# Loading r, k and v of the first four blocks as pairs of tokens in a fused time-mixing and feed-forward kernel

## The chip, the cores and the metric

The kernel runs on one core of a Trainium2 chip, in one launch. The metric is device time in microseconds (us): the median of several executions, lower is better. A profile is one further execution, recorded by the hardware profiler. Its span runs from the first to the last recorded instruction, and its own device time is a little longer than the span.

The engines are named as in the profile: PE does matrix multiplies (PEld loads their stationary operand), DVE is the vector engine, ACT the scalar engine, POOL the general-purpose one. SP computes nothing here; it issues most of the transfers (DMA) in the order of its own queue.

## The reference, cut to what matters

For each of 4 batches (index `j` in the kernel) and 8 heads there are 768 tokens with 48 channels a head. A recurrence over the tokens gives y, its rows are laid side by side over the heads to x (3072 rows of 384), and a gated feed-forward with 1536 hidden units follows.

```python
for t in range(S):                        # r, k, v, w: (4, 8, 768, 48); u: (8, 48)
    cur = einsum('bhd,bhe->bhde', u[None] * k[:, :, t], v[:, :, t])
    y[:, :, t] = einsum('bhd,bhde->bhe', r[:, :, t], state + cur)
    state = w[:, :, t][..., None] * state + einsum('bhd,bhe->bhde', k[:, :, t], v[:, :, t])
x = y.transpose(0, 2, 1, 3).reshape(B * S, H * D)
xn = x / sqrt(mean(x * x) + 1e-6) * rms_g
out = (silu(xn @ w_gate) * (xn @ w_val)) @ w_out
```

All inputs are float32 in HBM; the matrix multiplies of before take bfloat16 operands, but for two small ones (`u_mm`, `g_mm`), and add in float32.

## The kernel before, in words

**Blocks.** The work is cut into 24 blocks `(n, j)`: block `n` (0 to 5) of 128 tokens of batch `j` (0 to 3). Each block goes through the recurrence in chunked form. With the logarithms of w summed over the tokens of the block (`ln`, `cs_mm`), r is scaled by the exponential of the sum (`exp_r`, `r_mul`) and k by that of its negative (`exp_k`, `k_mul`). Both are transposed (`rk_pe` on PE and `rk_tr`, or, for n of 2 and more, `rk_tr` alone as a transposing DMA), scores of all token pairs are formed (`q_mm`, even heads in one PSUM bank and odd heads in another), masked to earlier tokens (`q_mask_e`, `q_copy_o`, `q_mask_o`), and y is scores times v plus r times the state from before the block (`y_mm`). `st_mm` and `st_new` make the new state. The term with u, which concerns a token itself, is made on the side: `bonus_mul` (two POOL multiplies), `bonus_sum` (DVE), `bonus_v` (POOL), which leaves the tile `ydiag`; `x_add` (DVE, L553) adds it to y out of PSUM into the tile `xb`. Then x is normed (`x_sq`, `x_rstd`, `xn_mul`), transposed (`xn_pe` and `xn_out`, or `xn_tr` and `xn_gain`) and waits in a tile `xnt`.

**Feed-forward groups.** Four blocks make a group of 512 rows: `gate_mm`, `silu`, `val_mm`, `h_mul` for each of 12 slices of the hidden units, then `o_mm`, `o_out`, `out_dma` for each of the four blocks. The first group consists of the blocks (0,0), (0,1), (1,0) and (1,1), so its first matrix multiply (L617) has to wait for these four blocks to be through. The later groups overlap with the recurrence of later blocks.

**Loads.** `load` (L259) brings r, k or v of one block into a tile of 128 partitions (tokens) by 8 heads by 48 channels: 192 KB, in 1024 runs of 192 bytes, since tokens lie 192 bytes apart within one head. Eight such tiles a tensor (`NIN`) rotate. `load_w` (L271) does the same, but for the blocks in the set `WIN` (n of 0 and 1, all four batches) it loads the 256 tokens of two blocks at once: partition p holds tokens 2p and 2p+1, in 1024 runs of 384 bytes. Sums over tokens then take two matrix multiplies, with two masks cut from `mw` (L404, L408, L411). r, k and v of those blocks are still laid out one token a partition. All loads, the transposing DMAs and the stores of the result go through SP's queue; the weights of the feed-forward (`load_gv`, `load_wo`) through POOL's.

**Order.** Nothing is reordered at build time. A text, `ORDER`, lists every step as `step.n.j`, and each engine runs its instructions in that order, waiting where an operand or a buffer is not there. A number behind a colon puts that many multiplies by a tile of zeros ahead of the step (L238 on three 128-column transposes each, L240 on 384 columns); their results are overwritten, and they fill time on PE. PSUM is split into two banks `a`, two banks `b` and four banks `q`; the function `psum` gives a step the bank whose last use lies furthest back. Sets such as `CAST_ACT`, `K_POOL`, `RK_DVE`, `ODD_DVE` and `OUT_DVE` say for each block which engine does a step.

Of the kernel before, what the change touches and what calls it, by code (L numbers as in the profile page):

```python
# [30 lines left out]
bonus_mul.1.0 q_mask_e.0.0 load_k.1.3 load_r.1.2 load_k.1.2 load_r.1.3 load_v.1.2 bonus_mul.0.1 load_w.2.1 load_w.2.0
load_v.1.3 load_w.2.3 q_mm.1.0:2 cs_mm.1.1 exp_r.1.1 exp_k.1.1 r_mul.0.1 k_mul.0.1 w_tot.0.1 q_mask_o.1.0
bonus_sum.1.0 load_gv.0.1 cast_v.0.1 load_r.2.0 bonus_sum.0.1 r_mul.1.1 load_w.2.2 rk_pe.0.1:2 ln.0.3 y_mm.0.0
rk_tr.0.1 st_mm.0.1:4 x_add.0.0 q_mask_e.1.0 st_new.0.1 cs_mm.0.3:3 bonus_v.0.1 cast_v.1.0 q_mm.0.1:1 y_mm.1.0
k_mul.1.1 bonus_v.1.0 cast_v.1.1 q_copy_o.0.1 x_sq.0.0 bonus_mul.1.1 load_r.2.1 x_add.1.0 exp_r.0.3 load_r.2.2
x_sq.1.0 load_r.2.3 load_k.2.0 q_mask_e.0.1 w_tot.1.1 rk_pe.1.1:1 rk_tr.1.1 q_mm.1.1:7 q_mask_o.1.1 load_gv.0.0
q_mask_o.0.1 y_mm.0.1:8 g_mm.0.0 bonus_sum.1.1 ln.0.2 x_rstd.1.0 xn_mul.1.0 x_rstd.0.0 xn_mul.0.0 exp_k.0.3
bonus_v.1.1 load_gv.1.0 q_mask_e.1.1 x_add.0.1 x_sq.0.1 x_rstd.0.1 y_mm.1.1 x_add.1.1 k_mul.0.3 xn_pe.1.0:2 xn_pe.0.0
cs_mm.0.2 g_out.0.0 xn_out.1.0 x_sq.1.1 xn_mul.0.1 xn_out.0.0 r_mul.0.3 st_mm.1.1:3 x_rstd.1.1 st_mm.1.0 xn_mul.1.1
xn_pe.0.1 xn_out.0.1 w_tot.0.3 rk_pe.0.3:3 xn_pe.1.1 xn_out.1.1 exp_r.0.2 exp_k.0.2 r_mul.0.2 val_mm.0.0:4 gate_mm.0.3  # L40
silu.0.3 val_mm.0.3 rk_tr.0.3 w_tot.0.2 st_new.1.1 load_gv.1.1 k_mul.0.2 bonus_mul.0.2 q_mm.0.3 h_mul.0.3 st_new.1.0
gate_mm.0.2 gate_mm.0.0 rk_pe.0.2 silu.0.0 silu.0.2 val_mm.0.2 q_mask_e.0.3 h_mul.0.0 gate_mm.0.5 gate_mm.0.1 silu.0.5
silu.0.1 val_mm.0.1 rk_tr.0.2 q_copy_o.0.3 h_mul.0.1 bonus_mul.0.3 bonus_sum.0.3 h_mul.0.2 gate_mm.0.6:1
gate_mm.0.11:1 q_mm.0.2 cast_v.0.2 silu.0.6 silu.0.11 q_mask_o.0.2 gate_mm.0.8 val_mm.0.6 q_mask_e.0.2 cast_v.0.3
st_mm.0.2 val_mm.0.11 q_mask_o.0.3 h_mul.0.6 val_mm.0.5 y_mm.0.3 y_mm.0.2 bonus_sum.0.2 bonus_v.0.2 load_wo.0.0
# [668 lines left out]
```

## Time and profile before

| | us |
|---|---|
| median of 3 runs (203.16 to 204.44) | 204.01 |
| the profiled execution, device time | 203.96 |
| its span | 202.2 |
| PE busy in it | 191.3 (95%) |
| DVE busy | 157.5 (78%) |
| ACT busy | 135.0 (67%) |
| POOL busy | 124.4 (62%) |

A line of the timeline gives start and duration in us, the engine, the source line, the operation, `out<-in` and how many instructions were merged into it; brackets at its end say how long the engine sat idle before it and for whom. Matrix multiplies are pipelined, so the time that one takes is read from the start of one line to the start of the next. In the table by stages each engine's entry is its busy time, with the number of instructions in brackets. SPq is SP's queue of transfers; its line starts when SP begins to issue.

### The profile page before, as it was taken

To read this page: it belongs to the slowest core of one execution; us is meant where nothing else is said; L and a number is where in the kernel's file an instruction comes from. 1 tells how busy PE (TensorE), PEld (TensorE's weight loads), DVE (VectorE), ACT (ScalarE), POOL (GpSimd) and SP (SyncE) were. 2 spreads that over 40 slices of the span, in tenths; PEclk is the share of its full clock that TensorE was granted. 3 is DMA by queue.
4 is the path that set the end of the run, shared out by engine and by line. 5 is a ranking of instruction groups with operands and counts; after the bars stand their busy time and mean duration, and the time that the engine had idled before them with its cause. 6 is when DMAs were issued, how large, how long until landed. Compare 5 with 4: busy or idle time off the path is not lost.

```text
span 202.2 us, 4604 instructions
## 1 busy us (share of the span) xinstructions
PE 191.3 (95%) x1677; PEld 121.9 (60%) x1694; DVE 157.5 (78%) x307; ACT 135.0 (67%) x278; POOL 124.4 (62%) x178
## 2 busy tenths in 40 slices
...
GB/s 144 231 234 207 212 208 202 195 179 208 206 184 225 160 212 191 210 185 188 199 176 215 237 188 203 183 190 108 134 179 104 0 23 99 0 117 0 63 115 99
DMA packets 121567, 32.42 MB, mean 160 GB/s; under 512 B 116420, under 2 KB 120392, under 8 KB 121544
## 3 DMA queue, kind: packets, MB, share of 16 engines
...
q10 hardware_dynamic: 8, 0.00, 0.0%
...
## 4 chain that ended last, share of the span: by engine, by line
PE 65%; ACT 3%; DMA 2%; DVE 2%; issue 1%; SPq 0%; DVEq 0%; ACTq 0%
PE ps_av L617 7%; PE ps_bu L617 7%; PE ps_au L617 7%; PE ps_bv L617 6%; PE ps_qx L660 6%; PE ps_qv L660 6%; PE ps_qu L660 5%; PE ps_qz L660 4%; PE ps_au L622 2%; PE ps_bu L622 2%; DMA rkT<-rk 2%; PE ps_av L622 2%; PE ps_bv L622 2%; ACT L249 1%; PE ps_au L419 1%; PE ps_qv L500 1%
## 5 line engine op out<-in xcount | busy, mean ns | idle before, releaser
L660 PEld LDWEIGHTS <-ht 128*128 128x128 bf16 x300 | 28.1, 98 | 17.5 <-DVE ht L646 1.0
L251 ACT ACTIVATE sg<-ps_av 128x512 bf16<-128x512 f32 x36 | 21.5, 597 | 22.8 <-PE ps_av L617 18.0
L646 DVE TENSOR_TENSOR ht<-ps_bv,sg 128x512 bf16<-128x512 f32 x29 | 19.9, 687 | 13.9 <-PE ps_bv L617 12.9
L251 ACT ACTIVATE sg<-ps_au 128x512 bf16<-128x512 f32 x36 | 21.5, 596 | 11.5 <-PE ps_au L617 7.7
L617 PEld LDWEIGHTS <-wg_sb 128*128 128x128 bf16 x180 | 19.2, 114 | 15.9 <-issue 0.6
L617 PEld LDWEIGHTS <-wv_sb 128*128 128x128 bf16 x180 | 19.2, 114 | 15.7 <-issue 0.5
L465 POOL TENSOR_TENSOR ruk<-rt,kt 128x384 f32<-128x384 f32 x24 | 24.0, 1001 | 3.7 <-DMA kt<-in_k_dram 2.8
L475 POOL TENSOR_TENSOR ydiag<-vt,diag 128x384 f32<-128x384 f32 x24 | 20.4, 859 | 9.4 <-DVE diag L470 9.1
L617 PE MATMUL ps_av<-xnt,wg_sb 128*128 128x512 bf16 x88 | 25.0, 381 | 0.3
L466 POOL TENSOR_TENSOR ruk<-ruk,u_bc 128x384 f32<-128x384 f32 x24 | 24.0, 1001 | 1.9
L617 PE MATMUL ps_bu<-xnt,wv_sb 128*128 128x512 bf16 x86 | 24.8, 380 | 0.4
L646 DVE TENSOR_TENSOR ht<-ps_bu,sg 128x512 bf16<-128x512 f32 x31 | 21.3, 686 | 4.8 <-PE ps_bu L617 3.1
L617 PE MATMUL ps_au<-xnt,wg_sb 128*128 128x512 bf16 x87 | 23.6, 380 | 0.1
L617 PE MATMUL ps_bv<-xnt,wv_sb 128*128 128x512 bf16 x82 | 23.2, 380 | 0.2
L459 POOL TENSOR_TENSOR rk<-kt,ek 128x384 bf16<-128x384 f32 x16 | 15.9, 1001 | 9.7 <-ACT ek L251 5.9
L249 ACT ACT_TABLE_LOAD x14 | 18.0, 1283 | 1.9 <-PEq L698 1.6
L660 PE MATMUL ps_qx<-wo_sb,ht 128*128 128x384 bf16 x96 | 17.1, 326 | 0.2 <-DVE ht L646 0.2
L558 ACT ACTIVATE junk<-xb 128x384 bf16<-128x384 f32 x24 | 12.5, 522 | 6.3 <-DVE xb L553 6.2
L571 ACT ACTIVATE xn<-xb,rstd 128x384 bf16<-128x384 f32 x24 | 14.2, 609 | 0.6 <-POOL rstd L567 0.5
L470 DVE TENSOR_REDUCE diag<-ruk 128x8 f32<-128x384 f32 x24 | 13.1, 544 | 1.9 <-POOL ruk L466 1.9
L660 PE MATMUL ps_qv<-wo_sb,ht 128*128 128x384 bf16 (+1 forms) x84 | 13.8, 314 | 0.0
L251 ACT ACTIVATE lw<-wt 128x384 bf16<-128x384 f32 (+1 forms) x20 | 11.6, 583 | 2.8 <-DMA wt<-in_w_dram 2.7
...
## 6 DMA issues: line engine op xcount, KB each, us to landing
rt<-in_r_dram SPq DMA_DIRECT2D x24, 192.0 KB, 4.0
vt<-in_v_dram SPq DMA_DIRECT2D x24, 192.0 KB, 3.9
kt<-in_k_dram SPq DMA_DIRECT2D x24, 192.0 KB, 3.9
out_dram<-ob SPq DMA_DIRECT2D x23, 192.0 KB, 2.2
wt<-in_w_dram SPq DMA_DIRECT2D x16, 192.0 KB, 3.7
...
```

Of the source, the lines that this page charges most:

```text
L249: nc.scalar.preload_act_table_set(table_name)
L251: return nc.scalar.activation(**kw).ins
L459: eng.tensor_tensor(out=rk[:, n % 2, j, 1, :, 0:D], in0=inp["k", n, j], in1=bank["cs_k", n, j][:, 0:DM].rearrange("p (h d) -> p h d", h=H) ...
L465: nc.gpsimd.tensor_tensor(out=ruk[n, j], in0=inp["r", n, j], in1=inp["k", n, j], op=ALU.mult)
L466: nc.gpsimd.tensor_tensor(out=ruk[n, j], in0=ruk[n, j], in1=u_bc, op=ALU.mult)
L470: nc.vector.tensor_reduce(out=diag[n, j].rearrange("p h o -> p (h o)"), in_=ruk[n, j], axis=mybir.AxisListType.X, op=ALU.add)
L475: nc.gpsimd.tensor_tensor(out=ydiag[n, j], in0=inp["v", n, j], in1=diag[n, j].to_broadcast([128, H, D]), op=ALU.mult)
L571: nc.scalar.activation(out=xn, in_=xb[n, j], func=AF.Copy, scale=rstd[n, j][:, 1:2])
L617: nc.tensor.matmul(ps, lhsT=units(ws, c, f), rhs=x[:, c, :], start=(c == 0), stop=(c == KC - 1))
L622: nc.tensor.matmul(ps[:, i * TS // 2:(i + 1) * TS // 2], lhsT=units(ws, c, f + i), rhs=x[:, c, cols], start=(i == 0 and c == 0), stop=(i = ...
L646: nc.vector.tensor_tensor(out=ht[n][:, f, :], in0=v, in1=sg, op=ALU.mult)
L660: nc.tensor.matmul(ps[:, cols], lhsT=ht[n][:, f, b * L:(b + 1) * L], rhs=wo_sb[:, f, cols], start=(f == 0), stop=(f == FC - 1))
```

## The change

Four blocks, (0,0), (0,1), (1,0) and (1,1), form a set `PAIR`. For them r, k and v are loaded as w was: one transfer of 384 KB for both blocks of a batch, 1024 runs of 384 bytes, partition p holding tokens 2p and 2p+1. Block 0 of such a pair then holds the even tokens and block 1 the odd tokens of all 256. What follows in consequence:

- `cs_mm` uses masks of whole token pairs (`mp`) and, for the sum over a chunk, a column that is one on the chunk's half of the partitions (`chunk_of`).
- `rk_tr` writes both blocks of a batch into one tile `rkTp`, sorted by chunk of 128 tokens. `q_mm` makes scores of one chunk at a time: 16 multiplies with 64 output rows in place of 8 with 128.
- `st_mm` and `y_mm` of chunk n take half of the rows (64 partitions) of both blocks, so 8 multiplies in place of 4 and 16 in place of 8.
- `yd_mm` is new: for these four blocks `ydiag` is added in PSUM by PE, through two float32 multiplies by a 64x64 part of an identity. `x_add` goes away for them; `x_sq` and `xn_mul` read the PSUM bank.
- `out_dma` of these blocks stores 64 even and 64 odd rows: the destination is 2 x 64 rows of 384 in place of 128 rows.

Beside this, r, k and v of all other blocks lie two batches to a tile (four tiles of 384 KB a tensor in place of eight of 192 KB; still one 192 KB transfer a block). Some buffer counts change (`ydiag` 6 to 5, `rkT` 6 to 5 beside two `rkTp`, `xb` 4 to 3, `qts` 3 to 4), `ORDER` is written anew throughout, and so are the sets that place steps on engines. Counted over the whole kernel, PE loses 24 zero multiplies of 384 columns and gains 3 of 128; DVE loses 4 `x_add`, 5 output copies, 2 transposed copies and 3 masks and gains 2 `k_mul`; ACT gains 5 output copies, 3 score copies and 2 transposed copies. The number of activation table loads, of feed-forward multiplies and of SP's steps for other blocks is the same. All transfers of the four blocks are issued by SP in the order `w.0 k.0 r.0 w.0.1 r.1 k.1 w.0.3 v.0 r.0.2 v.1`, where a single number is the batch of a pair.

```diff
-load_r.0.0 load_w.0.0 u_mm.0.0 ln.0.0 load_v.0.0 load_k.0.0 cs_mm.0.0:2 load_r.1.0 load_w.0.1 u_out.0.0 load_k.1.0
-load_k.0.1 load_w.0.3 load_v.0.1 exp_r.0.0 exp_k.0.0 r_mul.0.0 cast_v.0.0 load_r.0.1 bonus_mul.0.0 load_k.1.1
-bonus_sum.0.0 bonus_v.0.0 k_mul.0.0 cs_mm.1.0 load_r.1.1 load_v.1.1 load_v.1.0 load_w.0.2 rk_pe.0.0:2 rk_tr.0.0
-exp_r.1.0 w_tot.1.0 w_tot.0.0 st_mm.0.0 r_mul.1.0 st_new.0.0 q_mm.0.0:4 load_k.0.3 load_r.0.3 load_r.0.2 load_k.0.2
...
+load_w.0.0 ln.0.0 u_mm.0.0:12 u_out.0.0 load_k.0.0 load_r.0.0 bonus_mul.0.0 bonus_mul.1.0 load_w.0.1 load_r.0.1
+load_k.0.1 load_w.0.3 load_v.0.0 load_r.0.2 load_v.0.1 load_v.0.3 cs_mm.1.0 g_mm.0.0 cs_mm.0.0 exp_k.1.0 exp_r.1.0
+load_w.0.2 load_k.0.3 load_k.0.2 load_r.0.3 load_v.0.2 load_k.1.2 k_mul.1.0 r_mul.1.0 rk_pe.1.0:5 load_r.1.2 exp_k.0.0
+exp_r.0.0 k_mul.0.0 r_mul.0.0 w_tot.0.0 ln.0.1 rk_pe.0.0:2 w_tot.1.0 rk_tr.0.0 rk_tr.1.0 bonus_sum.0.0 cs_mm.0.1
+exp_r.0.1 g_out.0.0 r_mul.0.1 w_tot.0.1 exp_k.0.1 k_mul.0.1 cs_mm.1.1 q_mm.0.0 q_mm.1.0 load_v.1.2 load_r.1.3
+load_w.2.1 q_mask_e.0.0 load_k.1.3 bonus_sum.1.0 q_mask_o.0.0 bonus_mul.1.1 exp_k.1.1 k_mul.1.1 ln.0.3 rk_pe.0.1:1
+bonus_v.1.0 bonus_v.0.0 exp_r.1.1 load_w.2.0 q_mask_e.1.0 q_mask_o.1.0 cs_mm.0.3 cast_v.0.0 cast_v.1.0 load_v.1.3
+r_mul.1.1 load_w.2.2 load_w.2.3 load_r.2.1 load_r.2.0 rk_tr.0.1 w_tot.1.1 st_mm.0.0:3 bonus_sum.1.1 st_new.0.0
+load_gv.0.0 bonus_mul.0.1 y_mm.0.0 rk_pe.1.1 yd_mm.0.0 rk_tr.1.1 load_k.2.1 load_r.2.3 q_mm.0.1 x_sq.0.0 load_k.2.0
+q_copy_o.0.1 q_mask_e.0.1 bonus_sum.0.1 x_rstd.0.0 xn_mul.0.0 bonus_v.1.1 y_mm.1.0 cast_v.1.1 q_mm.1.1:1 q_mask_e.1.1
+q_mask_o.1.1 q_mask_o.0.1 cast_v.0.1 ln.0.2 yd_mm.1.0 bonus_v.0.1 load_gv.0.1 y_mm.0.1 exp_r.0.3 st_mm.0.1 st_new.0.1
+x_sq.1.0 x_rstd.1.0 yd_mm.0.1 load_gv.1.0 load_gv.1.1 cast_v.0.3 y_mm.1.1 xn_pe.0.0 yd_mm.1.1 cs_mm.0.2 xn_out.0.0
+w_tot.0.3 x_sq.0.1 xn_mul.1.0 exp_k.0.3 k_mul.0.3 x_rstd.0.1 xn_mul.0.1 xn_pe.0.1 x_sq.1.1 x_rstd.1.1 xn_mul.1.1
+xn_pe.1.0 st_mm.1.1 xn_pe.1.1:3 exp_r.0.2 exp_k.0.2 bonus_mul.0.3 bonus_mul.0.2 r_mul.0.3 xn_out.0.1 xn_out.1.0
+xn_out.1.1 rk_pe.0.3 st_mm.1.0 val_mm.0.2 gate_mm.0.0 w_tot.0.2 r_mul.0.2 k_mul.0.2 gate_mm.0.2 rk_pe.0.2 st_new.1.0
+rk_tr.0.3 silu.0.0 gate_mm.0.1 rk_tr.0.2 cast_v.0.2 silu.0.1 q_mm.0.3 val_mm.0.0 st_new.1.1 bonus_sum.0.2 silu.0.2
+q_mask_e.0.3 h_mul.0.0 q_mask_o.0.3 h_mul.0.2 st_mm.0.3 gate_mm.0.6 gate_mm.0.11 val_mm.0.1 st_mm.0.2 q_mm.0.2
+silu.0.6 silu.0.11 q_mask_e.0.2 val_mm.0.3 gate_mm.0.3 gate_mm.0.8 q_copy_o.0.2 q_mask_o.0.2 h_mul.0.1 bonus_sum.0.3
+bonus_v.0.3 bonus_mul.1.2 silu.0.3 h_mul.0.3 val_mm.0.11 h_mul.0.11 gate_mm.0.5 val_mm.0.6 h_mul.0.6 st_new.0.2
...
+bonus_sum.2.0 out_dma.0.3 rk_tr.2.2 gate_mm.1.0 o_out.0.1 silu.1.0 gate_mm.1.5 st_mm.2.1 val_mm.1.5 gate_mm.1.2
...
-    NIN, NRUK, NYD, NRKT, NE, NXB, NSG, NQT, NHT = 8, 3, 6, 6, 4, 4, 3, 3, 2
+    NIN, NRUK, NYD, NRKT, NE, NXB, NSG, NQT, NHT = 8, 3, 5, 5, 4, 3, 3, 4, 2
+    HL = L // 2
...
+    PAIR = sel("00 01 10 11")
...
+    YD_PE = sel("00 01 10 11")
...
-        inp[which, n, j] = pin.tile([128, H, D], FP32, name=which + "t", bufs=NIN)
+        if (n, j) in PAIR:
+            both = pin.tile([128, 2 * DM], FP32, name=which + "t", bufs=NIN // 2).rearrange("p (h x) -> p h x", h=H)
+            inp[which, 0, j], inp[which, 1, j] = both[:, :, 0:D], both[:, :, D:2 * D]
+            nc.sync.dma_start(out=both,
+                              in_=t[j, :, 0:2 * L, :].rearrange("h (p i) d -> p h (i d)", i=2))
+            return
+        if (which, n, j) not in inp:
+            both = pin.tile([128, 2 * DM], FP32, name=which + "t", bufs=NIN // 2).rearrange("p (b h d) -> p b h d", b=2, h=H)
+            a = j - j % 2
+            inp[which, n, a], inp[which, n, a + 1] = both[:, 0], both[:, 1]
...
+            if (n, j) in PAIR:
+                upto, total = (lambda i, own: mp[:, int(2 * i + 1 - own <= 2 * n)]), (lambda i: chunk_of[:, n:n + 1])
+            else:
+                upto, total = (lambda i, own: mw[:, n, i, own:L + own]), (lambda i: mw[:, n, i, L:L + 1])
...
+        if (n, j) in PAIR:
+            if (0, j) not in rkT:
+                rkT[0, j] = rkT[1, j] = pt.tile([128, 2 * NP, 2, 2, HL], BF16, name="rkTp", bufs=2)
+            out = rkT[n, j][:, :, :, n, :].rearrange("p q c x -> p (q c) x")
+            ps = bank.pop(("tr", n, j)).rearrange("p q (c x) -> p (q c) x", c=2)
...
+            if (n, c) in PAIR:
+                for i in range(NP):
+                    for a in range(2):
+                        for ps, d in ((qe, slice(0, D)), (qo, slice(PD, PD + D))):
+                            nc.tensor.matmul(ps[a * HL:(a + 1) * HL, i, :], lhsT=t[d, NP + i, a, n, :],
+                                             rhs=t[d, i, a].rearrange("p b x -> p (b x)"),
+                                             start=(i == 0), stop=(i == NP - 1))
+                continue
...
+            for m in parts:
+                nc.tensor.matmul(ps[:, i, :], lhsT=pair(rk[rows, m % 2, j, 1], i), rhs=pair(vb[m, j][rows], i),
+                                 start=(not old and i == 0 and m == parts[0]), stop=(i == NP - 1 and m == parts[-1]))
...
+    def yd_mm(n, j):
+        xb[n, j] = bank.pop(("y", n, j))
+        if (n, j) in PAIR:
+            rows = slice(n * HL, (n + 1) * HL)
+            for m in range(2):
+                nc.tensor.matmul(xb[n, j][m * HL:(m + 1) * HL], lhsT=ident32[rows, rows],
+                                 rhs=ydiag[m, j][rows].rearrange("p h d -> p (h d)"), start=False, stop=True)
+            return
+        nc.tensor.matmul(xb[n, j], lhsT=ident32, rhs=ydiag[n, j].rearrange("p h d -> p (h d)"), start=False, stop=True)
...
-        nc.sync.dma_start(out=out[row0:row0 + L, cols], in_=bank.pop(ob)[:, cols])
+        dst = out[row0:row0 + L, cols]
+        if (i, j) in PAIR:
+            dst = dst.rearrange("(x a) m -> a x m", a=2)
+        nc.sync.dma_start(out=dst, in_=bank.pop(ob)[:, cols])
```

More of the change, by code (lines that the diff above doesn't have):

```diff
@@ L31 @@
[L31 to L45, printed above, removed]
@@ new lines @@
+h_mul.0.5 h_mul.0.8 k_mul.1.3 gate_mm.0.7 gate_mm.0.9 rk_pe.1.2 bonus_sum.1.2 bonus_v.1.2 x_add.0.3 rk_tr.1.2
+x_add.0.2 cast_v.1.2 ln.2.1 silu.0.9 silu.0.7 val_mm.0.9 gate_mm.0.4 val_mm.0.4 rk_pe.1.3 rk_tr.1.3 x_sq.0.3 x_sq.0.2
+silu.0.4 q_mm.1.2 cs_mm.2.1 gate_mm.0.10 q_mm.1.3 q_copy_o.1.2 h_mul.0.9 x_rstd.0.2 bonus_mul.1.3 val_mm.0.10
+h_mul.0.4 silu.0.10 h_mul.0.10 val_mm.0.7 h_mul.0.7 q_mask_o.1.2 o_mm.0.2 q_mask_e.1.2 ln.2.0 x_rstd.0.3 xn_mul.0.2
+y_mm.1.2 cs_mm.2.0 cast_v.1.3 q_mask_o.1.3 cs_add.2.1 q_mask_e.1.3 exp_r.2.1 x_add.1.2 o_mm.0.3 y_mm.1.3 xn_pe.0.2
```

253 lines of the change are left out of this document (134 added, 119 removed).

## The prediction

> **What bounds the kernel now.** I read the busy time by stages first, then PE's timeline for what starts the dense stage, then the queue of transfers.
>
> ```profile
> core 0: us, PE busy (x) PEld busy (x) DVE busy (x) ACT busy (x) POOL busy (x), PEclk, DMA share, GB/s
> 0.00:11.00 11.00, 6.84 (x48) 3.93 (x49) 5.46 (x15) 5.13 (x8) 6.22 (x19) 1.00 0.86 187
> 11.00:30.20 19.20, 17.41 (x238) 12.23 (x236) 16.68 (x37) 12.92 (x32) 15.54 (x20) 1.00 1.13 216
> 30.20:199.10 168.90, 167.03 (x1394) 105.72 (x1409) 135.11 (x257) 116.92 (x239) 102.64 (x141) 1.00 0.73 153
> 199.10:202.20 3.10, 0.00 (x0) 0.00 (x0) 0.29 (x1) 0.00 (x0) 0.00 (x0) 0.86 0.28 98
> ```
>
> The stages are mine: 30.2 us is where the first feed-forward multiply starts. From there to 199.1 PE is busy 167.03 of 168.90 us: PE's own work bounds it, and neither a faster load nor a faster DVE shortens it. What can move the time is when that stage starts, whether PE stays fed in it, and the 3.1 us tail. The start, on PE:
>
> ```profile
> 4.16 1.64 PE L372 MATMUL ps_qu<-u_bc,ones_row 1*128 1x384 f32 x2 [4.16 <-POOL ones_row L338]
> 5.74 0.82 PE L240 MATMUL ps_au<-zero 128*128 128x384 bf16 x2
> 6.35 0.85 PE L404 MATMUL ps_au<-lw,mw 128*128 128x384 bf16 x2
> ...
> 7.84 0.84 PE L404 MATMUL ps_av<-lw,mw 128*128 128x384 bf16 x2
> ...
> 14.38 0.50 PE L404 MATMUL ps_av<-lw,mw 128*128 128x384 bf16 x2
> ...
> 15.25 0.50 PE L238 MATMUL ps_qv<-ident,zero 128*128 128x128 bf16 x6
> 15.58 0.61 PE L482 MATMUL ps_qv<-ident,rk 128*128 128x128 bf16 x8
> 16.03 0.36 PE L548 MATMUL ps_qz<-vb,qts 128*128 128x48 bf16 x8
> ...
> 16.96 0.33 PE L528 MATMUL ps_qu<-vb,rk 128*128 128x96 bf16 x4
> 17.13 0.65 PE L240 MATMUL ps_au<-zero 128*128 128x384 bf16 x3
> 17.62 0.49 PE L404 MATMUL ps_au<-lw,mw 128*128 128x384 bf16 x2
> ...
> 18.73 0.23 PE L500 MATMUL ps_qv<-rkT 48*128 48x128 bf16 x1
> ...
> 19.06 0.34 PE L545 MATMUL ps_qx<-st,rkT 128*128 128x96 bf16 x4
> ...
> 20.48 1.30 PE L240 MATMUL ps_qz<-zero 128*128 128x384 bf16 x7
> 22.64 0.23 PE L500 MATMUL ps_qz<-rkT 48*128 48x128 bf16 x1 [0.85 <-DVE rkT L489]
> ...
> 22.97 1.47 PE L240 MATMUL ps_qv<-zero 128*128 128x384 bf16 x8
> ...
> 29.23 0.33 PE L586 MATMUL ps_qz<-ident,xn 128*128 128x128 bf16 x3
> 29.40 0.81 PE L240 MATMUL ps_bv<-zero 128*128 128x384 bf16 x4
> 30.21 0.81 PE L617 MATMUL ps_bv<-xnt,wv_sb 128*128 128x512 bf16 x2
> ...
> 36.94 0.33 PE L240 MATMUL ps_av<-zero 128*128 128x384 bf16 x1
> ...
> 37.74 0.33 PE L240 MATMUL ps_au<-zero 128*128 128x384 bf16 x1
> ```
>
> From 11 to 30.2 us PE is busy too, but much of it is padding: the zero multiplies shown alone (3, 7, 8 and 4 of L240) come to 22 x 0.163 = 3.6 us (three take 17.62 - 17.13 = 0.49). The start waits for loads and for the chain of DVE, ACT and POOL behind them, while PE has room.
>
> ```profile
> 1.31 0.56 SPq L271 DMA_DIRECT2D wt<-in_w_dram  x1
> ...
> 13.51 1.82 SPq L259 DMA_DIRECT2D vt<-in_v_dram  x2
> 15.37 0.70 SPq L271 DMA_DIRECT2D wt<-in_w_dram  x1
> ```
> ```profile
> 8.47 0.50 ACT L387 CAST vb<-vt 128x384 bf16<-128x384 f32 x1
> ```
> ```profile
> 19.11 0.50 POOL L389 CAST vb<-vt 128x384 bf16<-128x384 f32 x1 [0.62 <-DMA vt<-in_v_dram]
> ```
>
> The last two loads of the four blocks are issued from 13.51 us on, and POOL sits waiting for one of them until 19.11 us.
>
> **Term 1, the loads.** Before needs 12 loads of 192 KB and 3 of w (384 KB) until then, 3.5 MB; at the 216 GB/s of the second stage that is 16 us, and with issue and landing it gives the 19. After needs 6 + 3 loads of 384 KB, and `r.0.2` stands ahead of the last: 3.7 MB. Run for run the traffic halves (6144 in place of 12288 for r, k, v). If bytes set the pace, v of batch 1 lands no earlier (19 us); if runs did, in 10 x 1024 of them in place of 15 x 1024 and so at two thirds of the time, it lands at 13. I take 17. But v of batch 0, whose first part is cast at 8.47 us in before, is now eighth in the queue: about half the list, so 13 to 15 us. Loads come 2 us earlier at the end and 6 us later in the middle.
>
> **Term 2, PE's work ahead of the first feed-forward multiply.** Here the change adds to PE. Up to the second `rk_pe`: ACT has w's logarithm at about 5 us, since w is now first in the queue. PE runs 12 zero multiplies at the slow early pace (two take 6.35 - 5.74 = 0.61, so 3.7 us from about 1.1) and `u_mm` (1.6 us): 6.4. The first `cs_mm` takes 7.84 - 6.35 = 1.5 at the slow pace: 8.0; `g_mm` 0.2, the second `cs_mm` 15.25 - 14.38 = 0.87 at full pace, two `rk_pe` of 0.45, and 21 zero transposes of 0.055 (six take 0.33): 1.2. That ends at 11.1 us. Then, until the first feed-forward multiply:
>
> - four `cs_mm` of 0.87: 3.5; three `rk_pe` of 0.45: 1.35; four transposes of xn of 0.17: 0.7; eight zero multiplies: 1.3.
> - four `st_mm`, twice the 17.13 - 16.96 = 0.17: 1.4. Four `y_mm` with 16 multiplies for 8, of 0.025 each: 0.4 each, and 0.17 for the state's part in two: 1.95.
> - four `q_mm`. The 8 of before take 19.06 - 18.73 = 0.33, as two run side by side in two halves of the array's rows. The 16 of after lie in four quarters. If four run side by side they cost 0.33, if only two do 0.66, if none does 1.3. I take 0.6, the case nearest to the row: 2.4.
> - four `yd_mm`, of two float32 multiplies with 384 columns each. The one row of this kind is `u_mm`: 5.74 - 4.16 = 1.58 us at the slow pace, at which bfloat16 took 0.305; halved for the full pace (0.163 for 0.305) it is 0.8. So 1.6 a block and 6.3 for four. The lower end is the bfloat16 multiply's 0.163 (1.3 for all eight). The upper would be 1.58 each, but that needs the slow pace, which the rows from 14 us on exclude, so 0.8 is the upper end too.
>
> The Trainium skill ("FP8 and Floating Point Precision", section TensorE Precision Notes) says that true float32 takes four passes through the array. That would make 4 x 0.163 = 0.65 a multiply and 5.2 us in all, 1.1 less than by the row; the row, 1.58 for 0.305, is 5.2 passes, and has its own start in it.
>
> Sum: 3.5 + 1.35 + 0.7 + 1.3 + 1.4 + 1.95 + 2.4 + 6.3 = 18.9 us, from 11.1 to 30.0; two short waits like those in the rows (0.85 at the longest) I count as 0.6. It starts at 30.6 us, against 30.21: **+0.4 us**. Bounds: with quarter overlap and the lower float32 price PE's list ends 6 us earlier, but then the chain behind the loads holds the start. Its end in before, from that last landing (19.11) to the multiply (30.21), is 11.1 us. After saves four `x_add` from it, of which the chain of one block passes one:
>
> ```profile
> 25.92 0.56 DVE L553 TENSOR_TENSOR xb<-ps_qx,ydiag 128x384 f32<-128x384 f32 x1 [0.30 <-PE ps_qx L548]
> ```
>
> So 17 + 11.1 - 0.56 = 27.5 at the earliest: -2.7. With `q_mm` at 1.3 the list is 2.8 longer: +3.2.
>
> **Term 3, the dense stage.**
>
> ```profile
> rt<-in_r_dram SPq DMA_DIRECT2D x24, 192.0 KB, 4.0
> ```
>
> The program order of both versions, counted by kind, shows the same multiplies left behind the first feed-forward multiply: all of the feed-forward and the recurrence of 20 blocks, with `cs_mm` of (0,3) and (0,2) and `rk_pe` of (0,3) done ahead of it in both. Only the two zero multiplies at 36.94 and 37.74 are gone: **-0.3 us**. DVE loses about 12 instructions and ACT gains 10; at 135 and 117 busy of 169 us neither becomes the bound, and PE's own work covers both. If that cover fails in places, the cost is unknown, since the order is new: from -1.9 (all of PE's idle time gone) to one load waited for in full (4.0 us from issue to landing, the row above). I take 0. The shared tiles for two batches come free later than single ones; the loads they hold back are those of blocks two rounds ahead, so 0 as well, within the same bound. The tail has the same half store at its end: 0, at most 0.4 either way.
>
> **Sum:** 203.96 (the profiled execution; 202.2 of span and 1.8 around it, 0.05 under the median) + 0.4 - 0.3 = 204.1; I forecast **204.2**.
>
> **Rivals.**
>
> *The stores of the four blocks crawl (slower).* The new destination is 2 x 64 rows in place of 128. If the transfer is shared out over engines by its outermost dimension, two engines carry it, not 16.
>
> ```profile
> out_dram<-ob SPq DMA_DIRECT2D x23, 192.0 KB, 2.2
> ...
> u_bc<-in_u_dram ACTq DMA_DIRECT2D x1, 1.5 KB
> g_row<-in_moe_rms_g_dram ACTq DMA_DIRECT2D x1, 1.5 KB
> ```
> ```profile
> GB/s 143 165 259 243 154 187 252 286 298 289 277 265 253 238 226 214 162 123 200 204 164 183 174 263 324 325 310 280 266 253 236 223 230 188 159 199 304 321 326 298
> ```
> ```profile
> q10 hardware_dynamic: 8, 0.00, 0.0%
> ```
> ```profile
> PE ps_qu L500 <- DMA rkT<-rk: 0.6, 1, 0.6
> ```
>
> ACT's queue, q10, carried u (one run) and g (three runs) alone: 8 packets, 4 of data and 4 more. One closing packet for each engine used makes exactly 4 if u used one engine and g three; 16 engines each would have made 32. The best 250 ns anywhere in 2 to 12 us moved 326 GB/s, 20.4 for each of 16 engines. Two engines need 98304 B / 20.4 = 4.8 us for a store that 16 do in 0.6 at that rate: 4.2 us more, in which every later load and transposing DMA, spread over all 16, waits on those two. SP's order puts `rk_tr.2.2`, needed by `q_mm`, right behind the store of (0,3). One such delay fully exposed gives 204.2 + 4.2 = **208.4**; all four 221; none 204.2. It decides once more than 2 us of one store outlast the lead that loads have. For it speaks q10, against it that in before PE waits once, 0.6 us, for a transfer, the last row, so transfers have some lead.
>
> The Trainium skill ("DMA: Bandwidth & Descriptors", section Why a DMA increments its semaphore by 16 and not by 1) states this rule: the engine count is the largest k up to 16 that divides the slowest dimension of both sides. With 2 and 128 that is 2, and with one and three runs it agrees with the 8 packets.
>
> *The start moves with the loads (faster).* If the float32 multiplies and quarters overlap, the start is at 27.5: 203.96 - 2.7 - 0.3 = **201.0**. For it: the last landing is earlier and 24 zero multiplies go. Against: the later v, and PE's list.
>
> *PE's new forms cost more.* `q_mm` without overlap: 204.2 + 2.8 = **207.0**. Against: the rows show two at a time.
>
> *The halved runs do nothing for the landing* (19 us in place of 17): PE's list still covers it, so 204.2 holds.
>
> **How the numbers follow.** Forecast (within 1%, which is about what a measurement here can tell from no change): 0.43, its own range 202.5 to 206. Slow stores 0.37, though part of it is hidden: some of these stay under 207. Dearer forms 0.05. Faster start 0.15. So faster by over 1% 0.15, within 0.43, slower 0.42. The range takes in most of the slow stores and half of the faster case: 201.5 to 209.5.
>
> **What would show it.** Term 1: POOL's or ACT's wait for vt of batch 1 ends near 17 us. Term 2: PE without long idle from 11 us on, `yd_mm` at 1.6 a block, first feed-forward multiply at 30 to 31. Term 3: about 169 us from there to the last output multiply. The slow stores would show as landings near 6 us in place of 2.2 on four stores, and PE waiting for transposed tiles or loads between 55 and 110 us. I am wrong if the first feed-forward multiply comes before 29, or if PE idles over 2 us in the dense stage.

## The result, and the profile after

The changed kernel takes **215.6 us** (median of 4, 213.8 to 216.7) against 204.2 for the kernel before beside it (203.2 to 204.4): 1.056 times as long, 95% interval 1.048 to 1.065. Ratios, here and below, leave out executions more than 1.5% above a kernel's fastest; where several were left out, the spread of all is given. The profiled execution took 216.74 us, its span 214.8, which is 12.6 us more than the span before. The same table by stages as in the prediction, now of the profile after; the second stage ends where the first feed-forward multiply starts:

```profile
core 0: us, PE busy (x) PEld busy (x) DVE busy (x) ACT busy (x) POOL busy (x), PEclk, DMA share, GB/s
0.00:11.00 11.00, 9.71 (x45) 4.59 (x46) 5.38 (x14) 3.28 (x5) 8.41 (x22) 1.00 0.93 254
11.00:34.46 23.46, 22.00 (x320) 15.41 (x317) 14.77 (x34) 17.27 (x39) 18.45 (x23) 0.85 1.09 211
34.46:211.70 177.24, 168.98 (x1395) 106.42 (x1408) 130.59 (x249) 120.61 (x247) 98.42 (x136) 0.99 0.70 138
211.70:214.80 3.10, 0.00 (x0) 0.00 (x0) 0.00 (x0) 0.12 (x1) 0.00 (x0) 0.96 0.19 63
```

Two stages lost time. The feed-forward starts at 34.46 in place of 30.21 (+4.25), and the dense stage takes 177.24 in place of 168.90 (+8.3). PE's idle time in the dense stage rose from 1.9 (168.90 - 167.03) to 8.3 us (177.24 - 168.98); the other 1.9 us are busy time, at a mean clock of 0.99 where before had 1.00. In the second stage the mean clock is 0.85. The waits of PE in the dense stage after (engine and line, what it waited for, us in total, times, longest):

```profile
PE ps_qx L535 <- DMA rkT<-rk: 2.1, 1, 2.1
PE ps_av L441 <- DVE wcol L468: 2.0, 1, 2.0
PE ps_qx L724 <- ACT ob L733: 0.7, 1, 0.7
```

The first, from 79.7 us on, is for a transposed tile. The second, from 125.7 on, is a cumulative sum held up by DVE, which stood waiting for a late load of r. The page of the profile after gives the packets of SP's queue, and the clock in 40 slices:

```profile
PEclk9999958999999999999999996999999999999999
q1 hardware_dynamic: 113208, 28.58, 64.9%
```

The packets count the engines. Before had 119504. The change removes 6144 runs and six transfers on 16 engines (96 closing packets), which leaves 113264; 56 are missing, and 56 = 4 stores x 14. So each of the four new stores used 2 engines, not 16. The records of single packets say the same: the 128 rows of the first of these stores, that of block (1,0), moved from 60.97 to 66.41 us, those of the next two took 4.9 and 4.7 us, while the late stores, with 16 engines, take 0.6. So do the trace's semaphore records: each of the four stores has 3 of them, where a store on 16 engines has 16, and the last of the 3 comes 6.7 to 7.2 us after the issue began.

PEclk's 5 in the sixth slice is new, and so is the 6 at 129 us. The same table of the profile after, now cut at the clock's own steps. PEclk is the third column from the end: 1.00 is full speed and 0.50 half. It also says 1.00 where the trace has no record of the clock; the first record here, at full speed, is at 13.15 us, and what PE did before is read from its rows further down.

```profile
23.39:26.81 3.42, 2.90 (x47) 1.57 (x43) 1.82 (x3) 3.36 (x10) 3.42 (x5) 1.00 1.23 225
26.81:30.22 3.41, 3.41 (x32) 1.46 (x28) 1.56 (x4) 2.60 (x9) 3.15 (x6) 0.50 1.08 162
30.22:33.63 3.41, 3.41 (x31) 2.90 (x30) 1.09 (x3) 2.84 (x5) 2.89 (x4) 0.50 1.12 204
```

For 6.83 us PE ran at half speed, just ahead of the dense stage: 3.4 us of full-speed work. The timeline of PE in the profile after shows it, and what the new forms cost:

```profile
6.89 0.82 PE L428 MATMUL ps_au<-lw,mp 128*128 128x384 bf16 x2
...
13.38 0.61 PE L501 MATMUL ps_qz<-ident,rk 128*128 128x128 bf16 x8
13.82 0.49 PE L428 MATMUL ps_av<-lw,mp 128*128 128x384 bf16 x2
...
15.62 0.24 PE L530 MATMUL ps_qu<-rkTp 48*64 48x128 bf16 x1
...
16.89 0.33 PE L242 MATMUL ps_qu<-ident,zero 128*128 128x128 bf16 x3 [0.63 <-DVE qts L547]
...
20.33 0.86 PE L610 MATMUL ps_qx<-ydiag,ident 64*64 64x384 f32 x4
21.50 0.21 PE L530 MATMUL ps_qu<-rkTp 48*64 48x128 bf16 x1 [0.31 <-ACT rkTp L517]
...
24.48 0.72 PE L601 MATMUL ps_qx<-vb,qts 64*128 64x48 bf16 x16 [0.52 <-ACT vb L407]
...
27.59 1.55 PE L610 MATMUL ps_qu<-ydiag,ident 64*64 64x384 f32 x4
...
34.46 0.84 PE L681 MATMUL ps_bu<-xnt,wv_sb 128*128 128x512 bf16 x2
```

The two multiplies of `cs_mm` take 0.82 us at 6.89 and 0.49 at 13.82, so PE ran slowly until about 13.15. `yd_mm` takes 0.86 us for both of its multiplies at full speed, 1.55 in the slow stretch.

The loads did get faster. The same 3 us, first before, then after:

```profile
5.00:8.00 3.00, 3.00 (x17) 1.24 (x16) 0.62 (x2) 1.32 (x2) 0.92 (x1) 1.00 0.99 200
```
```profile
5.00:8.00 3.00, 2.75 (x14) 1.14 (x14) 0.56 (x1) 0.00 (x0) 1.59 (x5) 1.00 1.17 324
```

200 GB/s became 324. By the packets' records the pair load of v of batch 1 is through at 14.4 us (its landing is recorded at 14.9), where in before POOL waited for a v until 19.11. Nothing in the start waited for it:

```profile
17.26 0.91 ACT L407 CAST vb<-vt 128x384 bf16<-128x384 f32 x2
```

### The profile page after: what moved, and what is told of

Read it like the earlier page. It is cut to its first block, busy times and chain, and to the rows that moved or that the text cites. A ratio compares the mean times of both kernels' runs of the same rounds, so it can differ in the third digit from the quotient of the medians.

```text
span 214.8 us, 4732 instructions
## 1 busy us (share of the span) xinstructions
PE 200.7 (93%) x1754; PEld 126.4 (59%) x1769; DVE 150.7 (70%) x296; ACT 141.3 (66%) x290; POOL 125.3 (58%) x180
## 4 chain that ended last, share of the span: by engine, by line
PE 57%; POOL 11%; SPq 9%; ACT 7%; DMA 6%; issue 5%; DVE 3%; POOLq 1%; DVEq 0%; ACTq 0%
PE ps_av L681 8%; PE ps_au L681 7%; PE ps_bu L681 7%; PE ps_bv L681 7%; SPq L284 4%; SPq L272 4%; PE ps_qx L724 4%; PE ps_qu L724 3%; DMA rt<-in_r_dram 3%; POOL ruk L484 2%; POOL ruk L485 2%; POOL xnt L666 2%; ACT L253 2%; DMA xnt<-xn 2%; DMA kt<-in_k_dram 2%
## 5 line engine op out<-in xcount | busy, mean ns | idle before, releaser
L255 ACT ACTIVATE sg<-ps_av 128x512 bf16<-128x512 f32 x37 | 22.1, 598 | 19.2 <-PE ps_av L681 14.5
L710 DVE TENSOR_TENSOR ht<-ps_bu,sg 128x512 bf16<-128x512 f32 x30 | 20.6, 686 | 19.2 <-PE ps_bu L681 15.3
L484 POOL TENSOR_TENSOR ruk<-rt,kt 128x384 f32<-128x384 f32 x24 | 24.6, 1025 | 9.4 <-DMA kt<-in_k_dram 5.4
L681 PE MATMUL ps_bv<-xnt,wv_sb 128*128 128x512 bf16 x87 | 24.2, 380 | 1.2 <-POOL xnt L666 0.6
L494 POOL TENSOR_TENSOR ydiag<-vt,diag 128x384 f32<-128x384 f32 x24 | 19.7, 831 | 5.3 <-DVE wcol L468 3.3
L724 PE MATMUL ps_qx<-wo_sb,ht 128*128 128x384 bf16 x108 | 19.0, 326 | 0.7 <-ACT ob L733 0.7
L562 POOL TENSOR_SCALAR_AFFINE_SELECT qts<-qts 128x512 bf16<-128x512 bf16 x16 | 10.0, 636 | 16.3 <-ACT qts L553 16.3
L478 POOL TENSOR_TENSOR rk<-kt,ek 128x384 bf16<-128x384 f32 x14 | 14.0, 1000 | 5.9 <-ACT ek L255 4.8
L255 ACT ACTIVATE lw<-wt 128x384 bf16<-128x384 f32 (+1 forms) x20 | 11.4, 581 | 2.7 <-DMA wt<-in_w_dram 2.7
L666 POOL TENSOR_TENSOR xnt<-xnt,gT 128x384 bf16<-128x384 bf16 x8 | 6.6, 828 | 9.6 <-DMA xnt<-xn 9.6
L724 PE MATMUL ps_qu<-wo_sb,ht 128*128 128x384 bf16 x60 | 12.0, 355 | 0.2 <-DVE xnt L660 0.2
```

Of the source, the lines that this page charges most:

```text
L255: return nc.scalar.activation(**kw).ins
L478: eng.tensor_tensor(out=rk[:, n % 2, j, 1, :, 0:D], in0=inp["k", n, j], in1=bank["cs_k", n, j][:, 0:DM].rearrange("p (h d) -> p h d", h=H) ...
L484: nc.gpsimd.tensor_tensor(out=ruk[n, j], in0=inp["r", n, j], in1=inp["k", n, j], op=ALU.mult)
L494: nc.gpsimd.tensor_tensor(out=ydiag[n, j], in0=inp["v", n, j], in1=diag[n, j].to_broadcast([128, H, D]), op=ALU.mult)
L562: nc.gpsimd.affine_select(out=qts[n, j][:, 1], in_=qts[n, j][:, 1], compare_op=ALU.is_gt, fill=0.0, base=0, pattern=[[0, NP], [1, 128]], c ...
L666: eng.tensor_tensor(out=x, in0=x, in1=gT.to_broadcast([128, KC, L]), op=ALU.mult)
```

## The experiments

**Theory A:** the stores of 2 x 64 rows, on two engines each, hold up what SP issues behind them; that is the dense stage's loss. **Theory B:** the start's loss is PE's clock, which halves where PE has too little to do. Rivals: the new order or the shared tiles (for A); the operands or the forms of the new multiplies (for B). All times are medians; "before" was run beside each and took 203.6 to 204.4.

**e1_split: the stores on 16 engines.**

```diff
-            dst = dst.rearrange("(x a) m -> a x m", a=2)
-        nc.sync.dma_start(out=dst, in_=bank.pop(ob)[:, cols])
+            dst, src = dst.rearrange("(x a) m -> a x m", a=2), bank.pop(ob)
+            for a in range(2):
+                nc.sync.dma_start(out=dst[a], in_=src[a * HL:(a + 1) * HL, cols])
```

> After, with the store of each of the four pair blocks written as two transfers of 64 rows in place of one of 2 x 64 rows; nothing else. Theory A (a store of 2 x 64 rows is carried by two DMA engines, and what SP issues behind it waits for them): q1's packets rise by about 56, from 113208 to 113264 and some closing packets for the four more transfers (16 each if each uses 16 engines: 64), the four stores land in about 2.3 us in place of 3.4 to 4.4, PE's waits of 2.3 us at 79.5 and 2.2 us at 125.5 shrink to under 0.5 each, the half-speed stretch from 129.2 to 132.6 goes, and the dense stage falls from 177.2 to 170 to 172 us: 208 to 211 in all. Rival A' (the new order, or tiles shared by two batches, cause the waits): the packets change, the waits stay within 1 us, 214 to 216. Either way the first feed-forward multiply stays at 34.5.

Measured: **207.3** (206.1 to 209.3), 8.3 us less than after; against before 1.014 (1.008 to 1.020). Its page and its dense stage:

```profile
q1 hardware_dynamic: 113328, 28.58, 66.2%
```
```profile
32.61:201.50 168.89, 167.34 (x1410) 105.99 (x1408) 130.32 (x248) 120.14 (x247) 98.47 (x136) 1.00 0.72 148
```
```profile
PE ps_av L681 <- POOL xnt L666: 0.5, 1, 0.5
```

113328 = 113264 + 64: all the missing closing packets are back, and 16 each for four more transfers. The dense stage is 168.89 us, before's 168.90, with no wait over 0.5 and no dip of the clock. Theory A holds, and the new order, the shared tiles and the smaller buffer counts cost the dense stage nothing that shows. The feed-forward's start, expected at 34.5 us, came at 32.61 in this profile (an execution of 206.1 us): the clock was full from 4.92 us and at half speed from 21.98 to 32.22.

**e8_before2: the same stores in the old kernel.**

```diff
-        nc.sync.dma_start(out=out[row0:row0 + L, cols], in_=bank.pop(ob)[:, cols])
+        dst = out[row0:row0 + L, cols]
+        if i < 2 and j < 2:
+            dst = dst.rearrange("(x a) m -> a x m", a=2)
+        nc.sync.dma_start(out=dst, in_=bank.pop(ob)[:, cols])
```

> The kernel before with one edit: the stores of the blocks (0,0), (0,1), (1,0) and (1,1) go to 2 x 64 rows, as in after, so that the rows of these four blocks land at exchanged places within their block. Theory A with any order: q1 has 56 packets fewer, the four stores land in 3.4 to 4.4 us, and PE or the loads wait: 207 to 212. If only the new order is hurt (a transposing DMA needed soon stands right behind the stores), 204 to 205.

Measured: **214.4**, 1.051 (1.045 to 1.057), outside of what either case expected. q1 has 119448 packets, 56 fewer than before. Waits in the dense stage:

```profile
PE ps_bu L617 <- ACT ek L251: 3.8, 1, 3.8
ACT ob L669 <- DMA out_dram<-ob: 3.3, 1, 3.3
ACT lw L251 <- DMA wt<-in_w_dram: 7.7, 3, 4.2
PE ps_av L419 <- ACT lw L251: 2.2, 1, 2.2
```

Four stores of this shape are alone worth 10.4 us in a kernel that has nothing else of the change. What SP issues behind them comes late: ACT waits 7.7 us for three loads of w, where in before it waits for none of them in the dense stage, and PE's waits of 2.2 and 3.8 us are for what ACT makes right behind two of these loads. The stores also hold the three `ob` tiles, but the longest wait for one, ACT's 3.3 us, ends at 98.7 us, and the load that PE's 3.8 us hang on (issued at 92.82) lands at 100.18. The clock is at half speed in this dense stage too, for 10.2 us in all, from 86.6 and from 100.2 us on.

**e2_ones, e3_hold: what the clock counts.** e2 fills the padding with ones (`memset(zero, 1.0)`), e3 adds padding:

```diff
-st_mm.0.1 ... y_mm.0.1 ... y_mm.1.1
+st_mm.0.1:2 ... y_mm.0.1:3 ... y_mm.1.1:2
```

> After, with the padding tile filled with ones in place of zeros; the padding's results are overwritten as before. Theory: the clock's monitor does not see multiplies whose operands are all zero (12 of them from 1.05 us on did not raise the clock before 13.15 us). Then the clock is full one or two of its 3.41 us steps sooner (6.3 or 9.7 us), and perhaps no half-speed stretch at 26.8; the first feed-forward multiply comes 1 to 4 us sooner and the time is 211 to 215. Rival (the monitor goes by instructions or passes, whatever the operands): the clock's changes stay at about 13 and 27 us but for the phase of its steps, and the time within 1 us of after's 215.6.

> After, with seven more zero multiplies of 384 columns between 23.4 and 26.8 us (two ahead of st_mm of (0,1), three ahead of y_mm of (0,1), two ahead of y_mm of (1,1)): 1.1 us more work on PE, of which 0.5 lies in a wait for ACT. Theory B (the clock halves at 26.8 us because PE has too little that its monitor counts in the step before): the half-speed stretch from 26.8 to 33.6 goes, and the first feed-forward multiply comes at 31.5 to 32.5 in place of 34.46; 212.5 to 214. Rival: the stretch stays (zeros do not count, or the float32 multiplies are what is missed), and the start is 0.5 us later: 216.

Measured: e2 **215.7**, as after: with ones in place of zeros nothing is gained. (Its clock was full at 5.8 us, e1's, with zeros, at 4.9: when the clock rises differs from execution to execution of the same early code.) e3 **212.1** (211.1 to 214.6), 3.5 us less with 1.1 us more work; so added zeros do keep the clock up, and that zeros are not counted is refuted. In e3's profile (an execution of 214.6 us) the feed-forward starts at 32.74 us, 1.7 before after's. The same steps of the clock in e3's profile, busy and at full speed:

```profile
23.39:26.81 3.42, 3.42 (x41) 1.43 (x35) 1.85 (x3) 3.27 (x9) 3.42 (x5) 1.00 1.11 193
26.81:30.22 3.41, 3.41 (x48) 2.10 (x47) 1.82 (x4) 2.89 (x8) 3.15 (x6) 1.00 1.07 167
```

**e5_bf16, e6_xadd: is it the float32 multiplies?** On top of e1, `yd_mm` in bfloat16, or undone:

```diff
+            flat = ydiag[n, j].rearrange("p h d -> p (h d)").bitcast(BF16)
+            ydiag[n, j] = flat[:, 0:DM].rearrange("p (h d) -> p h d", h=H)
...
-lhsT=ident32[rows, rows],
+lhsT=ident[rows, rows],
```
```diff
-    YD_PE = sel("00 01 10 11")
+    YD_PE = sel("")
...
-yd_mm.0.0 ... yd_mm.1.0 ... yd_mm.0.1 ... yd_mm.1.1
+x_add.0.0 ... x_add.1.0 ... x_add.0.1 ... x_add.1.1
```

> e1_split (207.3) with ydiag of the four blocks rounded to bfloat16 and yd_mm's two multiplies in bfloat16, still by 64x64 parts of the identity; the term with u is thereby rounded to 8 bits. PE loses 4 x 0.65 = 2.6 us of work, all of it float32. Theory B1 (the float32 multiplies keep PE occupied, but its clock's monitor counts little of them, and so the clock halves): the half-speed stretch after 20 us goes although PE has less to do, and the first feed-forward multiply comes at 28.5 to 30 in place of 32.6: 203 to 205. Theory B2 (the monitor goes by PE's idle gaps): the gaps grow by what PE loses, the stretch stays, the start is at 31 to 32.5: 206 to 207.5.

> e1_split (207.3) with yd_mm undone: x_add on DVE adds ydiag, in the places in which yd_mm stood, as in before. PE loses 3.2 us of float32 multiplies, DVE gains 4 x 0.56 us. B1: no half-speed stretch, start at 29.5 to 31.5, 204.5 to 206.5. B2: PE idles more, the stretch stays or grows, start at 33 to 34: 208 to 209.

In e6 the term with u is added to rows of other tokens, since only `yd_mm` sorts the rows. Measured: e5 **207.0** (204.7 to 209.1), e6 **209.2** (208.3 to 210.9), e1 207.3. Taking 2.6 us of float32 work off PE gained nothing that this can tell. In e5's profile:

```profile
20.93:24.35 3.42, 2.62 (x45) 1.98 (x44) 1.51 (x4) 3.35 (x9) 3.42 (x5) 0.50 1.10 204
24.35:27.76 3.41, 3.22 (x32) 1.85 (x33) 1.65 (x4) 2.83 (x9) 3.15 (x6) 0.50 1.04 168
27.76:31.17 3.41, 3.41 (x37) 2.73 (x36) 1.62 (x4) 3.18 (x7) 3.33 (x4) 0.50 1.15 208
```

Half speed for 10.2 us with no float32 in it, as long as in e1's profile. In e6, without `yd_mm` at all, it lasts as long:

```profile
20.93:31.17 10.24, 8.45 (x107) 6.79 (x107) 6.70 (x14) 9.38 (x24) 9.49 (x12) 0.50 1.11 186
```

That the new multiplies' number format starves the clock (B1) is refuted, and of the two theories B2 is left. Its start of 33 to 34 us did not come in e6, though: the feed-forward starts at 31.92, and the time is lost in the dense stage, where PE waits for POOL:

```profile
PE ps_bv L681 <- POOL xnt L666: 2.2, 1, 2.2
PE ps_av L681 <- POOL xnt L666: 1.3, 1, 1.3
```

I did not follow up why.

**e11_before_nopad: the same in the old kernel.** Before without the 15 zero multiplies `q_mm.1.1:7` and `y_mm.0.1:8`.

> The kernel before without the 7 zero multiplies ahead of q_mm of (1,1) and the 8 ahead of y_mm of (0,1): PE has 2.45 us less to do between 20 and 25 us. Theory B2 (the clock halves where PE has too little to do that its monitor counts, whatever the kernel): a half-speed stretch appears between 20 and 30 us, the first feed-forward multiply comes 1 to 4 us later, 205 to 208. Rival (it is something of the new forms, as 64-row multiplies): the clock stays full and the time at 203.5 to 204.2.

Measured: **205.7** (204.6 to 207.1), 1.011 (1.005 to 1.016): 2.45 us of work less, 2.1 us more time than before beside it, and the feed-forward starts at 31.71 in place of 30.21.

```profile
22.01:25.43 3.42, 1.18 (x20) 0.93 (x21) 2.66 (x6) 3.19 (x9) 3.33 (x5) 1.00 0.93 169
25.43:28.85 3.42, 3.42 (x37) 2.73 (x38) 2.77 (x7) 2.27 (x8) 2.79 (x5) 0.50 1.10 160
```

A step with 1.18 us busy, and the next at half speed, with none of the new forms. In both kernels the clock falls or stays up as padding is taken out or put in, as B2 says.

**e7_split_hold: both mends** (e1's and e3's edits).

> e1_split and e3_hold together (stores of 64 rows, and seven more zero multiplies between 23.4 and 26.8 us). If the two causes are separate, their gains add: 215.6 - 8.3 - 3.5 = 203.8, between 203 and 205, no half-speed stretch after the start and no wait of PE over 1 us in the dense stage. If the two share a cause, 206 to 207.

Measured: **204.9** (202.3 to 206.8), 0.997 (0.993 to 1.002). Of the change's 11.4 us, the stores are 8.3 and the clock's step 2.4; 0.7 is left, within the spread. The two gains nearly add (2.4 us for the padding here, 3.5 without the other mend), and with both mended the change can't be told from before. Five of the ten executions took 202.3 to 204.0 us and five 205.8 to 206.8. The mean clock is no guide to this (0.992 to 0.999 against 0.999 to 1.000), since it counts as full what comes before its first record. In the profile, of an execution of 206.8 us, that record is at 13.60 us; in e9b's below, of one of 203.8 with a mean of 0.992, it is at 4.31, with half speed from 7.73 to 11.14. So the early clock may make the spread; with one trace of e7 this is not shown.

**e9_start, e9b_cast, e12_pad: is more to be had from the start?** On top of e7: e9b moves one POOL cast, e9 also moves u's multiply off the head of PE's list (and sets the row of ones for it first), e12 is e9 with padding put back.

```diff
-x_rstd.0.1 xn_mul.0.1 ... cast_v.0.3 y_mm.1.1
+x_rstd.0.1 cast_v.0.3 xn_mul.0.1 ... y_mm.1.1
...
-u_mm.0.0:12 u_out.0.0 ... bonus_mul.0.0 bonus_mul.1.0 ... cs_mm.1.0 g_mm.0.0 cs_mm.0.0
+cs_mm.1.0:11 cs_mm.0.0 u_mm.0.0 g_mm.0.0
...
-rk_pe.1.0:5 ... w_tot.0.0 ln.0.1 rk_pe.0.0:2
+rk_pe.1.0:1 ... w_tot.0.0 u_out.0.0 ln.0.1 rk_pe.0.0:2 bonus_mul.0.0 bonus_mul.1.0
```
```diff
-cs_mm.1.0:11 ... rk_pe.1.0:1 ... rk_pe.0.1:1 ... rk_pe.1.1 ... q_mm.1.1:1 ... xn_pe.0.0
+cs_mm.1.0:13 ... rk_pe.1.0:4 ... rk_pe.0.1:6 ... rk_pe.1.1:4 ... q_mm.1.1:3 ... xn_pe.0.0:2
```

> e7_split_hold (204.9) with the order ahead of the first feed-forward multiply mended: ones_row is set first on POOL, u_mm stands behind the first two cs_mm, which have waited behind it and twelve zero multiplies until 6.9 us although w's logarithm is there at 5.0; u_out and the first bonus_mul follow; the POOL cast of v of (0,3), which waits for a late load ahead of a small multiply that the norm of (0,1) needs, stands behind that multiply. Theory C (the loads have left the chain, and what holds the start in after is the order on PE and POOL): the first scores come 1.5 to 2 us sooner and the first feed-forward multiply 1 to 2 us sooner than in e7_split_hold (32.86), 202.5 to 204, which would be faster than both kernels. Rival: another chain (ACT's copies and norms) holds it, and the time stays at 204 to 205.

> e7_split_hold with only the cast of v of (0,3) moved behind the small multiply of the norm of (0,1) on POOL, which in the chain of waits of e7_split_hold waited for that load until 27.3 us. If that wait holds the start: 0.5 to 1 us less, 204. If not, e7_split_hold's 204.9 within 0.5.

> e9_start with padding put back where its profile shows PE in a wait or on the way to one: 2 more zero multiplies ahead of the first cs_mm, 3, 5 and 4 more sets of three zero transposes ahead of rk_pe of (1,0), (0,1) and (1,1), 2 more zero multiplies ahead of q_mm of (1,1), 2 sets of transposes ahead of xn_pe of (0,0). Theory B2: the mean clock of all executions is 0.99 or more and the spread from 203 to 211 closes: median 202.5 to 204.5. Rival (the clock of e9_start falls for another reason): executions of 209 remain, median 206 to 209.

Measured: e9b **203.8** (202.3 to 206.1), 0.999 (0.996 to 1.003): nothing that can be told from before or, within its spread, from e7. e9 **209.0**, but from 203.2 to 211.5 over 12 executions. Its profiled execution was the best one, with a full clock throughout:

```profile
29.86 0.84 PE L681 MATMUL ps_bu<-xnt,wv_sb 128*128 128x512 bf16 x3
```

There the start is 0.35 us ahead of before's. Seven of the other executions, from 208.95 on, have mean clocks of 0.957 to 0.975. e12 **204.6** (203.3 to 205.3), 1.003 (1.001 to 1.006): with the padding back, twelve executions lie within 2 us, at mean clocks of 0.998 to 1. So padding decides the spread (B2 again). e12's start, 30.64 us, is 2.2 ahead of e7's profiled 32.86, but in e7's trace the clock came late (13.60). e9b and e13 (below) leave u's multiply where it was and start as early, at 30.71 and 30.72, with a clock full from about 4.3 us but for one step at half speed. By the time, 204.6 against 204.9, theory C's gain of 1 to 2 us is not there. No version here beats both kernels.

**e4_runs192, e10_hold192, e13_heads: what the longer runs are worth.** Each pair load in two transfers of 192 byte runs, on after (e4) and on e7 (e10); e13 has two transfers, of four heads each, with 384 byte runs, on e7.

```diff
-            nc.sync.dma_start(out=both,
-                              in_=t[j, :, 0:2 * L, :].rearrange("h (p i) d -> p h (i d)", i=2))
+            for i in range(2):
+                nc.sync.dma_start(out=inp[which, i, j],
+                                  in_=t[j, :, 0:2 * L, :].rearrange("h (p i) d -> p i h d", i=2)[:, i])
```
```diff
+            for hs in (slice(0, H // 2), slice(H // 2, H)):
+                nc.sync.dma_start(out=both[:, hs],
+                                  in_=t[j, hs, 0:2 * L, :].rearrange("h (p i) d -> p h (i d)", i=2))
```

> After, with each pair load of r, k and v issued as two transfers, one for the even and one for the odd tokens, in runs of 192 bytes in place of 384; the tiles, their contents and everything else are those of after. Tells what the longer runs alone are worth. If packets set the pace, the rate while r, k and v of the first blocks come in falls from 320 to about 200 GB/s, the last of these loads lands near 19 us in place of 15, and the start is late: by 0 if the chain on ACT, DVE and POOL behind the loads has 4 us of room, by 3 to 4 if it has none. I expect 1 to 3: 217 to 219. If bytes set the pace, the rate stays above 300 and the time within 1 us of after's.

> e7_split_hold with each pair load as two transfers of 192 byte runs (as e4_runs192 was to after): what the longer runs are worth once the stores and the clock are mended. Theory C (loads are off the chain): within 1 us of e7_split_hold, 204 to 206, though the last of these loads lands some 4 us later. Rival (the clock hid their worth): 2 to 4 us more, 207 to 209.

> e7_split_hold with each pair load as two transfers of four heads each, in runs of 384 bytes: as many transfers as e10_hold192, runs as long as in after. If the length of the runs is what e10_hold192 lost by: within 1 us of e7_split_hold, 204 to 205.5. If the number of transfers that SP issues: like e10_hold192, 206.5 to 208.

Measured: e4 **216.2** (214.2 to 219.1), 0.6 us above after and within its spread, below the 217 to 219 that I expected. e10 **207.3** (205.5 to 215.2), 1.017 (1.012 to 1.022), where two of seven executions, the profiled one among them, took 214 to 215 us at a mean clock of 0.944; e13 **204.8** (202.7 to 206.6), 1.002 (0.999 to 1.005), as e7. From 2 to 14 us, e10's and then e13's profile:

```profile
2.00:14.00 12.00, 11.12 (x138) 7.03 (x137) 8.32 (x18) 6.51 (x11) 8.21 (x16) 1.00 1.12 240
```
```profile
2.00:14.00 12.00, 11.47 (x119) 7.68 (x121) 7.44 (x15) 6.31 (x11) 9.26 (x17) 0.86 1.12 293
```

The number of transfers costs nothing that shows; the length of the runs is worth some 2.5 us on e7. On after itself it does not show; that the stores and the clock hide it there is argued, not shown. I had expected the loads to be off the chain in e10 too: that was wrong.

## Why the prediction was wrong

- **Forecast 204.2, range up to 209.5; measured 215.6.** The likeliest case left out two losses, of 8.3 and about 3 us.
- **The stores.** The mechanism was written down as a rival, with the right engine count; the step that failed is term 3, "I take 0", for waits in the dense stage. The rival's own price for one delay fully exposed, 208.4, was short too; for all four it named 221. In after, two delays of about 2 us are exposed (the waits of 2.1 and 2.0 us); the rest, to the measured 8.3, is smaller waits and a second half-speed step, at 129 us, that follows the second wait. The lead of the loads, which I held against this rival, did not last: DVE waits 3.4 us for a load of r ahead of the second wait, and in e8 ACT waits 7.7 us for loads of w. The Trainium skill ("DMA: Bandwidth & Descriptors", Why a DMA increments its semaphore by 16 and not by 1) had the count, and the 56 missing packets agree with it; the evidence beside it (q10's 8 packets) deserved more than 0.37. The sign foretold, landings near 6 us, came: 6.7 to 7.2 us by the semaphore records. The page's times from issue to landing, 4.4 at most, do not hold these four stores. The other sign, PE waiting between 55 and 110 us, came once in that stretch; the second wait is at 125.7, behind the last of the four.
- **Term 1, the loads** (17 us): too late. v of batch 1 is through at 14.4, nearer to the 13 of runs setting the pace than to the 19 of bytes; with runs twice as long the rate went from 200 to 324 GB/s, not to twice.
- **Term 2, PE's list** (start at 30.6, 34.46 measured in this execution). Two pieces were dearer on paper than on the chip: `q_mm` took 1.2 us for the four blocks in place of 2.4 (0.24 for the first; all four quarters run at once), and `yd_mm` 3.2, counted at full speed, in place of 6.3 (its two multiplies start 7 ns apart in the trace and run side by side, in two column halves); that is 4.3 us less. What failed is "full pace" from about 8 us on. The clock was full from 13.15 us, so the second `rk_pe` ended at 13.8 and not at 11.1 (+2.7, of which 0.5 were lost by 8.5 us, where I had counted the slow pace too); it halved from 26.8 to 33.6 (+3.4). The waits that PE shows before that come to 1.5 (0.63 + 0.31 + 0.52), where I counted 0.6 (+0.9), and the four `y_mm` took about 2.5 at full speed in place of 1.95 (+0.6). That adds to 30.6 - 4.3 + 2.7 + 3.4 + 0.9 + 0.6 = 33.9; the last 0.6 us I can't place. When the clock first becomes full is luck of the execution (13.15 us here, 4.92 in e1 with the same early code); that it halved again is for want of padding, as e3 shows. No rival had the clock in it, although the change takes 24 zero multiplies out, and I had called them padding.
- **Term 3, the order and the tail:** right but for the waits. With the stores mended, the dense stage is 168.89 for 168.90 (the forecast 0.3 less does not show); the tail is 3.1 in both.
- **Rivals.** The start that moves with the loads (201.0) did not come: its bound of 27.5 took the loads for the only thing ahead of the start, but with the loads early and the clock full (e9's best execution, in another order) PE starts at 29.86. Dearer forms: the opposite. Halved runs that do nothing for the landing: wrong (14.4 for 19.11 us), though in after itself they bring no time that shows.

What stays open: how much work in a step is enough. In before, a step with PE busy for 2.56 of 3.41 us was not followed by half speed:

```profile
20.40:23.81 3.41, 2.56 (x26) 1.42 (x24) 2.56 (x6) 2.60 (x8) 3.33 (x5) 1.00 1.17 218
```

In after, one with 2.90 was. The busy time of the profile is not the measure, and no run here finds which is.
